# Spacing the score maxima of the early heads in an attention and feed-forward kernel on one core

## The chip, the cores and the metric

The kernel runs on one core of one Trainium2 chip. The metric is the device time of one execution in microseconds, from the runs' own clock; a profile of one more execution tells where the time lies.

## What is computed

Four batches of eight heads (768 positions, 64 values each) go through attention with a hashed mask: six sign bits of q and of k by a random projection give a bucket each, and a score counts only where the buckets agree. The heads' outputs, side by side, go through a feed-forward layer of 512 to 2048 to 512 with a piecewise quadratic activation.

```python
q_bits = (np.einsum('bhsd,dk->bhsk', q, proj) > 0)
mask = q_bucket[:, :, :, None] == k_bucket[:, :, None, :]
scores = np.where(mask, scale * np.matmul(q, k.transpose(0, 1, 3, 2)), -1000000000.0)
scores = scores - np.max(scores, axis=-1, keepdims=True)
attn = np.exp(scores)
attn = attn / (np.sum(attn, axis=-1, keepdims=True) + 1e-09)
x = np.matmul(attn, v)                       # 32 heads, then 3072 tokens x 512
h = x @ w_in
g = np.where(h >= 1, h, np.where(h <= -1, 0.0, (h + 1) ** 2 / 4))
out = g @ w_out
```

## The kernel before

All products are made from float32 values split into a high and a low part in TensorE's faster float32 format. Attention comes first, the feed-forward layer after it; the order of all work is written out by hand, so each engine and each DMA queue works through its instructions in the order of the program.

Attention runs over 384 units, twelve for each of 32 heads. A unit (number g) is one block of 128 keys against one half (384) of the queries of a head: unit g belongs to head g // 12, to half 0 in its first six units and half 1 in the others. In each pass of the main loop (from L609) TensorE makes the scores of unit g (`s_unit`, two matmuls, L371 and L372, into one of four score banks `ps_s`), ScalarE takes the exponential twice (L380, L385), VectorE or, for two of six blocks, GpSimd takes the difference of the two as the low part (`lo_unit`, for unit g - 1), and TensorE adds the product with the values of unit g - 4 (`pv_unit`, three matmuls, L404 to L406, into `obank[0]` or `obank[1]`). So a unit is five matmuls of 128x384. Two heads form a pair, whose operands `T1` and `T2` are in one of three sets. A row of `T2` holds the negative maximum of each query, and the bits of the hash, so that mask and maximum are part of the scores' second matmul, L372.

The maxima of a head are found before: six times, for 128 queries each, two matmuls (`max_mm`, L310) write a tile `smax` of two banks, of which there is one only, and VectorE reduces it (`max_red`, L314) in the next pass, behind `s_unit`. Where they stand is in the table `early` (L604 to L608) for heads 0 to 5, up to unit 47; from unit 48 on one is made in every even unit, for the head two further on, always at the end of the unit. When a head's six are there, they are clamped (`max_clamp`), transposed on TensorE into `obank[1]` (`max_tr`), copied by ScalarE and sent by DMA to their row of `T2` (`max_put`, L356) and, as flags, to DRAM (L357). For head 2 this is done in two halves (`half_clamp`, `half_put`, L337 and L338; put at units 19 and 25), whose first needs the first three maxima alone. Heads 0 and 1 get their rows in another way (`row_half`).

All large DMAs are issued by SyncE, in the order of the program. Around the change these are, for each pair: the load of the next pair's raw q and k (`load_raw`, L147), four moves between `T1` and `T2` (`move`, L163), the load of v (`load_v`, L286), four small DMAs of the bits (`bits_put`, L282), and the results of a head (L416, L417). For pair 2 the first two moves stand at unit 16, the third at 19, `load_raw` for pair 3 at 20, the fourth move and `load_v` at 24, `bits_put` at 25. For pair 3, made while heads 2 and 3 run, GpSimd splits the raw values at units 26 to 29 (`cast_h`, `low_h`), the moves are at 29 and 32, `load_raw` at 33. From pair 4 on (g0 the first unit of the pair two before it): split at g0 to g0 + 3, moves at g0 + 3 and + 6, `load_raw` at + 7, bits on TensorE (`bits_mm`, L210, eight matmuls) at + 7 and + 11, `bits_put` at + 18; there max_put stood at g0 + 5 for the odd head (as head 5 at unit 53) and at g0 + 17 for the even one (head 6 at 65). Conversions of the feed-forward weights are spread over the units too.

Of the kernel before, what the change touches and what calls it, by code (L numbers as in the profile page):

```python
# [110 lines left out]
NU = 2 * NJ  # L111


def attention(ctx, tc, wst, T1, T2, qk, v, pj, cv, x_d, s_d, e_d, tasks, shared):
# [148 lines left out]
    def row_half(hd, hf, bank=None):  # L263
        ps = ps_m.tile([P, 2, 512], F32, name="smax")[:, 0] if bank is None else obank[bank]
        row_mm(hd, hf, ps)
        nc.scalar.copy(out=T2[0][32:33, 0, hd, hf * HS:(hf + 1) * HS], in_=ps[32:33, 0:HS])
# [54 lines left out]
    def half_clamp(hd, hf):  # L321

        nm = nms[hd]
        x = nm[:, hf * HB:(hf + 1) * HB]
        nc.vector.tensor_scalar(out=nmh[:, hf, HB:2 * HB], in0=x, scalar1=CLAMP, scalar2=None, op0=ALU.is_gt)
        nc.vector.tensor_scalar(out=nmh[:, hf, 0:HB], in0=x, scalar1=CLAMP, scalar2=None, op0=ALU.min)

    def half_put(hd, hf, bank):
        pr, h = hd // 2, hd % 2
        if hf == 1:  # L330
            nms.pop(hd)
        ps = obank[bank]
        nc.tensor.transpose(out=ps[0:2 * HB, 0:P], in_=nmh[:, hf], identity=ident)
        te = small.tile([2 * NJ, P], F32R, name="te")[0:2 * HB]
        nc.scalar.copy(out=te, in_=ps[0:2 * HB, 0:P])
        sl = slice(hf * HS, (hf + 1) * HS)
        nc.sync.dma_start(out=T2[pr % NQK][7:8, 0, h, sl].bitcast(F32), in_=te[0:HB].bitcast(F32))  # L337
        nc.sync.dma_start(out=e_d[hd // H][hd % H:hd % H + 1, sl], in_=te[HB:2 * HB].bitcast(F32))  # L338
# [8 lines left out]
    def max_tr(hd, bank):  # L347
        ps = mx[hd] = obank[bank]
# [46 lines left out]
    def pv_unit(n):  # L395
# [8 lines left out]
        nc.tensor.matmul(out=o, lhsT=wa, rhs=ph, start=(jj == 0), stop=False)  # L404
        nc.tensor.matmul(out=o, lhsT=wb, rhs=ph, start=False, stop=False)  # L405
        nc.tensor.matmul(out=o, lhsT=wa, rhs=pl, start=False, stop=(jj == NJ - 1))  # L406
# [126 lines left out]
    at(9, ones_row, 1, nc.vector)  # L533
# [5 lines left out]
    at(7, row_clamp, 1, 0, NJ // 2)  # L539
# [3 lines left out]
    at(9, bits_cmp, 1, 0)  # L543
    at(9, row_half, 1, 0)
# [18 lines left out]
    at(18, half_clamp, 2, 0)  # L563
    at(19, half_put, 2, 0, 1)
    at(23, half_clamp, 2, 1)
    at(25, half_put, 2, 1, 0)
    at(2 * NU + 1, lambda: nc.gpsimd.memset(T2[0][32:33, 0].bitcast(F32), 0.0))
    for hd in range(NH):
        pr, h = hd // 2, hd % 2
        g = hd * NU  # L570
        if 0 < hd < NH - 2:
            gc, gt = ((g + NU + 6, g + NU + 7) if hd == 1 else (g + NU + 2, g + NU + 4) if hd == 2
                      else (g + NU, g + NU + 4))
            at(gc, max_clamp, hd + 2, nc.gpsimd if hd > 2 else nc.vector)
            at(gt, max_tr, hd + 2, 1)
            at(gt + (hd > 1), max_put, hd + 2)
# [27 lines left out]
    early = {}  # L604
    for hd, gs in ((0, (0, 2)), (1, (4, 5, 6, 8, 11, 12)), (2, (15, 16, 17, 19, 20, 22)),
                   (3, (21, 23, 24, 26, 27, 29)), (4, (30, 31, 33, 34, 35, 37)),
                   (5, (38, 39, 41, 42, 44, 46))):
        early.update({n: (hd, NJ - len(gs) + i) for i, n in enumerate(gs)})  # L608
    for g in range(NG + LAG + 1):  # L609
        if g < NG:  # L610
            s_unit(g)
        if red is not None:
            max_red(*red)
            red = None
        if 1 <= g <= NG:
            lo_unit(g - 1)
        if g < 4 * NU:
            due = g in early
            hd, i = early.get(g, (0, 0))
        else:  # L620
            hd, i = g // NU + 2, g % NU // 2
            due = hd < NH and g % 2 == 0
        if g >= LAG and g - LAG < NG:
            pv_unit(g - LAG)
        if due:
            max_mm(hd, 2 * i)
            max_mm(hd, 2 * i + 1)
            red = (hd, i)
        for fn, a in tasks.pop(g, ()):
            fn(*a)  # L630
    for g in sorted(tasks):
# [652 lines left out]
```

## Time and profile before

| | us |
|---|---|
| median of 3 runs | 981.41 |
| lowest and highest run | 980.84, 982.14 |
| profiled execution, from the first to the last instruction | 980.2 |
| TensorE busy in it | 966.7 (99%) |
| VectorE, ScalarE, GpSimd busy | 793.9, 679.6, 346.3 |

The profiled execution's span is 1.2 us under the median of the runs, which is what lies around it. Attention takes the first 460 us or so, the feed-forward layer the rest. In the profile PE is TensorE, PEld its loading of weights, DVE VectorE, ACT ScalarE, POOL GpSimd and SPq the queue of SyncE. A matmul's printed duration (0.34 us for 384 columns) overlaps the next one's: they follow each other at about half of it. The clock granted to TensorE is at its full level throughout.

### The profile page before, as it was taken

How to read it: one execution, taken by the hardware profiler on the slowest of the kernel's cores; microseconds unless marked ns; L12 is line 12 of the kernel's file. 1: busy time of each engine (PE TensorE's matmuls, PEld its weight loads, DVE VectorE, ACT ScalarE, POOL GpSimd, SP SyncE). 2: the span in 40 equal slices, each digit the busy share in tenths (PEclk: the TensorE clock that was granted, in tenths of full speed). 3: DMA queues.
4: the chain of work that ended last, by engine and by line, in shares of the span. 5: the costliest groups of instructions: out<-in, count | busy, mean ns of one | idle time of the engine just before them, and what ended most of it. 6: DMA issues, size and time to landing. Idle time of an engine off the chain costs nothing.

```text
span 980.2 us, 15590 instructions
## 1 busy us (share of the span) xinstructions
PE 966.7 (99%) x5050; PEld 889.7 (91%) x5050; DVE 793.9 (81%) x1359; ACT 679.6 (69%) x1481; POOL 346.3 (35%) x418
## 2 busy tenths in 40 slices
PE   8999999999999999999999999999999999999998
PEld 7889999999999999999999998888988889988886
DVE  8779999999999999887898887877866777655554
ACT  7878988898899898888655555455564545544444
POOL 8767777778887777666000000000000000000000
PEclk9999999999999999999999999999999999999999
DMA  6674667676666667644395478966458554454431
GB/s 164 178 189 108 165 175 184 192 180 192 168 159 162 177 174 187 161 119 126 126 319 185 129 237 287 314 223 205 116 157 240 149 183 119 143 159 119 117 88 65
DMA packets 95113, 167.56 MB, mean 171 GB/s; under 512 B 13956, under 2 KB 51960, under 8 KB 95032
## 3 DMA queue, kind: packets, MB, share of 16 engines
q1 hardware_dynamic: 94808, 166.56, 59.6%
q8 instruction: 40, 0.66, 0.3%
q14 instruction: 41, 0.34, 0.1%
q10 hardware_dynamic: 224, 0.00, 0.0%
HBM read 106.13 MB, written 33.87 MB: 143 GB/s over the span
## 4 chain that ended last, share of the span: by engine, by line
PE 87%; DVE 5%; ACT 3%; DMA 2%; issue 1%; POOL 1%; SPq 1%; DVEq 0%; ACTq 0%; POOLq 0%
PE y L822 27%; PE h L1054 18%; PE smax L310 7%; PE h L959 7%; PE o L406 5%; PE o L404 5%; PE o L405 5%; PE s L371 5%; PE s L372 5%; DVE nm L314 2%; PE o L210 2%; DVE pl L39 1%; DMA wraw<-in_w_in_dram 1%; ACT ph L380 1%; DMA sm<-sd 0%
## 5 line engine op out<-in xcount | busy, mean ns | idle before, releaser
L380 ACT ACTIVATE ph<-s 128x384 fp32r<-128x384 f32 x380 | 188.3, 496 | 41.1 <-PE s L372 35.1
L314 DVE TENSOR_REDUCE nm<-smax 128x1 f32<-128x768 f32 x189 | 179.0, 947 | 15.2 <-PE smax L310 13.6
L39 POOL TENSOR_TENSOR pl<-pf,ph 128x384 fp32r<-128x384 f32 x128 | 141.9, 1112 | 87.8 <-ACT pf L385 83.1
L787 DVE SCALAR_TENSOR_TENSOR t<-t 128x384 f32<-128x384 f32 x128 | 71.3, 557 | 101.6 <-ACT z L782 101.3
L39 DVE TENSOR_TENSOR pl<-s,ph 128x384 fp32r<-128x384 f32 x256 | 135.8, 544 | 10.8 <-ACT s L385 9.6
L371 PE MATMUL s<-t 128*128 128x384 f32 x384 | 132.2, 344 | 0.0
L404 PE MATMUL o<-ph,va 128*128 128x386 f32 x384 | 130.1, 339 | 1.1 <-DVE neg L221 1.1
L406 PE MATMUL o<-pl,va 128*128 128x386 f32 x384 | 130.1, 339 | 0.4 <-DVE pl L39 0.4
L405 PE MATMUL o<-ph,vb 128*128 128x386 f32 x384 | 130.1, 339 | 0.0
L372 PE MATMUL s<-t 128*128 128x384 f32 x384 | 129.3, 337 | 0.0
L385 ACT ACTIVATE s<-s 128x384 f32<-128x384 f32 x252 | 125.2, 497 | 0.0
L822 PE MATMUL y<-t,ghi 128*128 128x512 f32 x384 | 124.7, 395 | 0.0
L310 PE MATMUL smax<-t 128*128 128x384 f32 x378 | 103.1, 354 | 5.7 <-DVE nm L314 4.4
L781 ACT ACTIVATE t<-h,mh 128x384 f32<-128x384 f32 x56 | 32.6, 581 | 84.0 <-PE h L959 44.3
L310 PEld LDWEIGHTS smax<-t 128*128 128x128 f32 x378 | 64.4, 188 | 23.8 <-DVE nm L314 22.1
L792 ACT CAST ghi<-z 128x384 fp32r<-128x384 f32 x129 | 65.1, 505 | 30.1 <-DVE z L788 26.3
L782 ACT ACTIVATE z<-t,m 128x384 f32<-128x384 f32 x128 | 79.0, 617 | 4.2
L1054 PE MATMUL h<-wbig,t 128*128 128x384 f32 x399 | 81.4, 336 | 0.0
L822 PEld LDWEIGHTS y<-t,ghi 128*128 128x128 f32 x384 | 71.3, 188 | 11.1 <-ACT ghi L792 0.3
L1054 PEld LDWEIGHTS h<-wbig,t 128*128 128x128 f32 x399 | 71.6, 188 | 5.3
L781 ACT ACTIVATE t<-wsq,mh 128x384 f32<-128x384 f32 x48 | 29.6, 617 | 67.0 <-DVE wsq L1067 40.8
L822 PE MATMUL y<-t,glo 128*128 128x512 f32 x192 | 76.0, 396 | 0.0
(189 smaller groups left out, 2134.9 us busy)
## 6 DMA issues: line engine op xcount, KB each, us to landing
t<-wc SPq DMA_DIRECT2D x92, 256.0 KB
t<-t SPq DMA_DIRECT2D x60, 384.0 KB
wraw<-wc SPq DMA_DIRECT2D x76, 256.0 KB
raw<-in_qk_dram SPq DMA_DIRECT2D x14, 768.0 KB
wraw<-in_w_in_dram SPq DMA_DIRECT2D x16, 512.0 KB
wraw<-in_w_out_dram SPq DMA_DIRECT2D x16, 512.0 KB
t<-ed SPq DMA_DIRECT2D x36, 192.0 KB
xd<-xs SPq DMA_DIRECT2D x32, 192.5 KB
```

The lines of the kernel that those rows point to most:

```text
L39: eng.tensor_tensor(out=out, in0=a, in1=b, op=ALU.subtract)
L310: nc.tensor.matmul(out=smax[hd][:, hf, 0:HS], lhsT=t2[:, 0, h, i * P:(i + 1) * P], rhs=t2[:, 1, h, hf * HS:(hf + 1) * HS], start=True, sto ...
L314: nc.vector.tensor_reduce(out=nmp(hd)[:, i:i + 1], in_=smax[hd][:, :, 0:HS], axis=AX.XY, op=ALU.max, negate=True)
L371: nc.tensor.matmul(out=ps[:, 0:HS], lhsT=t1[:, 1, h, ks], rhs=t1[:, 0, h, sl], start=True, stop=False)
L372: nc.tensor.matmul(out=ps[:, 0:HS], lhsT=t2[:, 1, h, ks], rhs=t2[:, 0, h, sl], start=False, stop=True)
L380: nc.scalar.activation(out=ph[:, 0:HS], in_=ps[:, 0:HS], func=AF.Exp, scale=SCALE)
L385: nc.scalar.activation(out=pf, in_=ps[:, 0:HS], func=AF.Exp, scale=SCALE)
L404: nc.tensor.matmul(out=o, lhsT=wa, rhs=ph, start=(jj == 0), stop=False)
L405: nc.tensor.matmul(out=o, lhsT=wb, rhs=ph, start=False, stop=False)
L406: nc.tensor.matmul(out=o, lhsT=wa, rhs=pl, start=False, stop=(jj == NJ - 1))
L822: nc.tensor.matmul(out=ys[c][m], lhsT=g_[:, m * P:(m + 1) * P], rhs=w, start=(first and k == 0), stop=(last and k == 2))
L1054: nc.tensor.matmul(out=ps, lhsT=w[:, cs], rhs=x, start=(n == 0 and s not in (2, 3, 6)), stop=(n == 5), skip_group_check=True)
```

## The change

The maxima of heads 0 to 5 are placed by a count of matmuls, five for a unit, and no longer by units only: `between(k)` is called behind the scores and behind each of the three value matmuls, and makes a maximum where `early` names the place 5 g + k. Those of heads 2 to 5 begin at place 80 (unit 16) and stand 7.7 places apart, up to unit 51; those of later heads keep one in two units, four units later than before (`SHIFT`). A maximum inside a unit is reduced at once, one at its end behind the next `s_unit`, as before.

The rows of heads 2 to 4 are now made in halves (clamps at units 19, 24, 29, 34, 38, 43, puts at 21, 26, 31, 36, 40, 45), clamped by GpSimd and no longer by VectorE; those of later heads are transposed at g + 18 and put at g + 19, counted from the first unit g of the head two before, in place of g + 16 and g + 17. Transposes and the row of head 1's first half go to a tile of the score banks and no longer to `obank` or `smax`. `ones_row` comes behind the compare of the bits in unit 9, a clamp of head 1 one unit later.

```diff
+SHIFT = 4
     def row_half(hd, hf, bank=None):
-        ps = ps_m.tile([P, 2, 512], F32, name="smax")[:, 0] if bank is None else obank[bank]
+        ps = ps_s.tile([P, 512], F32, name="s") if bank is None else obank[bank]
...
-        nc.vector.tensor_scalar(out=nmh[:, hf, HB:2 * HB], in0=x, scalar1=CLAMP, scalar2=None, op0=ALU.is_gt)
-        nc.vector.tensor_scalar(out=nmh[:, hf, 0:HB], in0=x, scalar1=CLAMP, scalar2=None, op0=ALU.min)
+        nc.gpsimd.tensor_scalar(out=nmh[:, hf, HB:2 * HB], in0=x, scalar1=CLAMP, scalar2=None, op0=ALU.is_gt)
+        nc.gpsimd.tensor_scalar(out=nmh[:, hf, 0:HB], in0=x, scalar1=CLAMP, scalar2=None, op0=ALU.min)
-    def half_put(hd, hf, bank):
+    def half_put(hd, hf):
...
-        ps = obank[bank]
+        ps = ps_s.tile([P, 512], F32, name="s")
...
-    def max_tr(hd, bank):
-        ps = mx[hd] = obank[bank]
+    def max_tr(hd, bank=None):
+        ps = mx[hd] = ps_s.tile([P, 512], F32, name="s") if bank is None else obank[bank]
...
         nc.tensor.matmul(out=o, lhsT=wa, rhs=ph, start=(jj == 0), stop=False)
+        between(3)
         nc.tensor.matmul(out=o, lhsT=wb, rhs=ph, start=False, stop=False)
+        between(4)
         nc.tensor.matmul(out=o, lhsT=wa, rhs=pl, start=False, stop=(jj == NJ - 1))
...
-    at(9, ones_row, 1, nc.vector)
...
-    at(7, row_clamp, 1, 0, NJ // 2)
+    at(8, row_clamp, 1, 0, NJ // 2)
...
     at(9, bits_cmp, 1, 0)
+    at(9, ones_row, 1, nc.vector)
...
-    at(18, half_clamp, 2, 0)
-    at(19, half_put, 2, 0, 1)
-    at(23, half_clamp, 2, 1)
-    at(25, half_put, 2, 1, 0)
+    for hd, gs in ((2, (19, 21, 24, 26)), (3, (29, 31, 34, 36)), (4, (38, 40, 43, 45))):
+        for n, g in enumerate(gs):
+            at(g, half_put if n % 2 else half_clamp, hd, n // 2)
...
-        if 0 < hd < NH - 2:
-            gc, gt = ((g + NU + 6, g + NU + 7) if hd == 1 else (g + NU + 2, g + NU + 4) if hd == 2
-                      else (g + NU, g + NU + 4))
-            at(gc, max_clamp, hd + 2, nc.gpsimd if hd > 2 else nc.vector)
-            at(gt, max_tr, hd + 2, 1)
-            at(gt + (hd > 1), max_put, hd + 2)
+        if 2 < hd < NH - 2:
+            at(g + NU + SHIFT - 1, max_clamp, hd + 2, nc.gpsimd)
+            at(g + NU + SHIFT + 2, max_tr, hd + 2)
+            at(g + NU + SHIFT + 3, max_put, hd + 2)
...
-    early = {}
-    for hd, gs in ((0, (0, 2)), (1, (4, 5, 6, 8, 11, 12)), (2, (15, 16, 17, 19, 20, 22)),
-                   (3, (21, 23, 24, 26, 27, 29)), (4, (30, 31, 33, 34, 35, 37)),
-                   (5, (38, 39, 41, 42, 44, 46))):
-        early.update({n: (hd, NJ - len(gs) + i) for i, n in enumerate(gs)})
+    order = [(0, 4), (0, 5)] + [(hd, i) for hd in range(1, 6) for i in range(NJ)]
+    places = [5, 15] + [25, 33, 40, 48, 55, 62] + [80 + 77 * n // 10 for n in range(4 * NJ)]
+    early = {n + (n % 5 == 1): hi for n, hi in zip(places, order)}
+    for hd in range(6, NH):
+        early.update({5 * ((hd - 2) * NU + SHIFT + 2 * i + 1): (hd, i) for i in range(NJ)})
     for g in range(NG + LAG + 1):
+
+        def between(k):
+            if 5 * g + k in early:
+                hd, i = early.pop(5 * g + k)
+                max_mm(hd, 2 * i)
+                max_mm(hd, 2 * i + 1)
+                if k == 5:
+                    return hd, i
+                max_red(hd, i)
+
         if g < NG:
             s_unit(g)
         if red is not None:
             max_red(*red)
...
             lo_unit(g - 1)
+        between(2)
         if g >= LAG and g - LAG < NG:
-            pv_unit(g - LAG)
-        if due:
-            max_mm(hd, 2 * i)
-            max_mm(hd, 2 * i + 1)
-            red = (hd, i)
+            pv_unit(g - LAG, between)
+        red = between(5)
```

## Rows read from the trace of the kernel before

**Rows 1.** The page, busy time of TensorE: us, share of the span, instructions.
```profile
PE 966.7 (99%) x5050; PEld 889.7 (91%) x5050; DVE 793.9 (81%) x1359; ACT 679.6 (69%) x1481; POOL 346.3 (35%) x418
```
**Rows 2.** Busy time by stretch: units 12 to 23, 24 to 47, 48 to 71.
```profile
28.50:46.80 18.30, 17.28 (x94) 14.89 (x93) 14.54 (x25) 14.60 (x34) 12.80 (x16) 1.00 0.64 152
46.80:79.80 33.00, 30.49 (x165) 27.66 (x164) 26.65 (x40) 25.36 (x60) 18.20 (x20) 1.00 0.66 170
79.80:107.70 27.90, 27.81 (x156) 26.50 (x155) 26.71 (x39) 25.15 (x61) 21.07 (x24) 1.00 0.63 166
```
**Rows 3.** Waits of TensorE from 29 to 80 us: sum, times, longest, us.
```profile
PE smax L310 <- DVE nm L314: 3.5, 13, 1.1
```
**Rows 4.** Timeline of TensorE, units 29 to 30: start, duration, what, idle before.
```profile
54.98 0.34 PE L406 MATMUL o<-pl,va 128*128 128x386 f32 x1
55.49 0.61 PE L310 MATMUL smax<-t 128*128 128x384 f32 x2 [0.18 <-DVE nm L314]
55.94 0.34 PE L371 MATMUL s<-t 128*128 128x384 f32 x1
```
**Rows 5.** Timeline of VectorE, units 9 to 10 and 30 to 31.
```profile
24.61 0.70 DVE L191 MEMSET t<- 1x768 f32 x1 [0.19 <-PE smax L260]
25.34 0.55 DVE L221 TENSOR_TENSOR neg<-o,neg 32x384 f32<-32x384 f32 x1
...
55.82 0.87 DVE L342 TENSOR_SCALAR nm<-nm 128x6 f32<-128x6 f32 x1
...
57.05 0.95 DVE L314 TENSOR_REDUCE nm<-smax 128x1 f32<-128x768 f32 x1
```
**Rows 6.** Timeline of TensorE, unit 10 and the first unit of head 2 (24).
```profile
25.94 0.44 PE L404 MATMUL o<-ph,va 128*128 128x386 f32 x1 [1.05 <-DVE neg L221]
...
47.00 0.34 PE L372 MATMUL s<-t 128*128 128x384 f32 x1
```
**Rows 7.** Timeline of SyncE's queue, DMAs issued in units 15 to 22.
```profile
32.85 0.52 SPq L163 DMA_DIRECT2D t<-t  x1
...
36.56 0.52 SPq L163 DMA_DIRECT2D t<-t  x1
...
41.55 1.13 SPq L337 DMA_DIRECT2D t<-te  x1
...
44.02 0.59 SPq L147 DMA_DIRECT2D raw<-in_qk_dram  x1
```
**Rows 8.** DMA packets from 44.6 to 45.6 us, and from 49.1 to 49.5 us.
```profile
DMA packets 69, 0.22 MB, mean 221 GB/s; under 512 B 22, under 2 KB 34, under 8 KB 69
...
DMA packets 4, 0.02 MB, mean 46 GB/s; under 512 B 1, under 2 KB 1, under 8 KB 4
```
**Rows 9.** The page, DMA issues: what, times, size of one.
```profile
t<-t SPq DMA_DIRECT2D x60, 384.0 KB
...
raw<-in_qk_dram SPq DMA_DIRECT2D x14, 768.0 KB
```
**Rows 10.** Timeline of GpSimd, units 25 to 31.
```profile
49.56 1.38 POOL L567 MEMSET t<- 1x1536 f32 x1
...
56.60 0.51 POOL L152 CAST t<-raw 128x384 fp32r<-128x384 f32 x1
```
**Rows 11.** Timeline of SyncE's queue, units 55 to 70.
```profile
88.49 1.16 SPq L163 DMA_DIRECT2D t<-t  x2
...
92.63 0.50 SPq L163 DMA_DIRECT2D t<-t  x1
...
103.96 3.33 SPq L282 DMA_DIRECT2D t<-bits  x4
```
**Rows 12.** Timeline of TensorE, the first L372 of heads 5 and 6.
```profile
94.89 0.34 PE L372 MATMUL s<-t 128*128 128x384 f32 x1
...
107.91 0.33 PE L372 MATMUL s<-t 128*128 128x384 f32 x1
```
**Rows 13.** Timeline of TensorE near the end of attention, unit 376.
```profile
454.89 0.44 PE L406 MATMUL o<-pl,va 128*128 128x386 f32 x1 [0.36 <-DVE pl L39]
```

## What I expect the change to do to the time

> **What bounds the kernel now.** I began with the page: TensorE is busy for 966.7 of the 980.2 us, at a granted clock of 1.00 in every stretch that I read [rows 1, 2]. So only two things move the time: matmuls added or removed (none here) and time in which TensorE waits. I then read the stretches. From unit 48 on, 156 instructions take 27.90 us, one each 0.179 us. In units 24 to 47 there are 165 in 33.00 us (0.200), in units 12 to 23 there are 94 in 18.30 us (0.195). At 0.179 these would have taken 29.5 and 16.8 us: 3.5 and 1.5 us are lost, 5.0 in all [rows 2]. The list of waits names the loss: 13 times TensorE waited for the reduction of the maxima before [rows 3]. The timeline shows one such wait [rows 4]: L406 starts at 54.98, the next matmul at 55.49 and not at 55.16, and the pair after it takes 0.45 us and not 0.36. That is 0.42 us in all, though the printed idle time is 0.18, because a matmul's end overlaps the next one's start.
>
> This loss is what the spacing can win. A maximum needs two matmuls and 7.7 others, 9.7 x 0.179 = 1.74 us from one to the next; a cycle through the single two-bank tile takes 0.61 us for the pair [rows 4] and 0.95 us for its reduction [rows 5], 1.56 us. So it fits, with less than 0.2 us left for VectorE being late.
>
> **Part by part, up to unit 24.** The compare at 25.34 stands behind a memset of 0.70 us [rows 5]; `ones_row` now comes behind it, so that the wait of 1.05 us at unit 10 [rows 6] shrinks by about 0.9. Of the 1.5 us lost in units 12 to 23 I give back 1.2. Maxima up to unit 24 are 14 in place of 16, which moves 4 x 0.179 = 0.7 us to later. With 0.5 us for head 1's maxima (they too are spaced now), unit 24 could begin about 3.3 us earlier, its second matmul at 43.7 in place of 47.00 [rows 6].
>
> It can't, by the queue of SyncE. That second matmul (L372) reads the first half row of head 2, which a DMA brings. Before, the row (L337) is issued at 41.55, ahead of the pair's last move and of the 768 KB load of `raw` at 44.02 [rows 7, 9]. `half_put` moves from unit 19 to 21; the last move of the pair stays at 19 and `load_raw` at 20. So the row is now issued behind both. What that means is in the packets: 12 of 512 bytes (34 under 2 KB less 22 under 512 B; the row and the flags have 6, the flags of head 1 the other 6) run between 44.6 and 45.6, some three microseconds after issue, behind the moves that had been issued just before. Then the last move and the load follow, whose last large packets are still running between 49.1 and 49.5 [rows 8]. The queue's order is the order of arrival. The row would thus come behind those last packets; with about 0.5 us for completion, 50.0 at the old pace. What feeds this queue starts with the bits of pair 1, whose compare comes only a few tenths earlier, since a reduction now precedes it; I take 0.4 us off for this and 0.3 for the two small DMAs that are no longer ahead: 49.3 to 50.0, taken 49.7. TensorE then idles from 43.7 to 49.7, and stands 2.7 us later at this matmul than before. The ends: 0 (the row is there in time, first rival) and 50.5.
>
> [...]
>
> **Units 24 to 47.** Now 120 matmuls of units, 30 of 15 maxima, 8 of bits and 5 transposes: 163 x 0.179 = 29.2 us. To it I add 0.05 us for each of the 15 maxima (0.7), and a new wait at unit 31: head 3's clamp goes to GpSimd, behind three of the four casts of units 26 to 28. They begin after a memset at 49.56 that itself follows unit 24, and the fourth cast starts at 56.60, 9.6 us after unit 24's L372 [rows 6, 10]. The clamp takes its place there and ends 0.5 us later, so 59.8 in the new time; the transposition at the end of unit 31 would be due at about 58.8 (49 matmuls x 0.179 after 49.7, and a few short waits): 1.0 us. In sum 30.9 us in place of 33.0, so unit 48 starts 2.7 - 2.1 = 0.6 us later than before. By then 29 maxima are done in place of 32; three come later, 6 x 0.179 = 1.1 us. Taking `max_clamp` off VectorE (0.87 us of the slow row [rows 5]) is in these figures. The halves of heads 3 and 4 add two transpositions, two copies and four DMA issues; ScalarE and SyncE have room.
>
> **The steady part, 22 heads from 5 to 26.** Maxima stay at the same even units, so VectorE's load is as before. The row is now issued two units later. For an odd head this is behind the pair's third move, for an even one behind the four DMAs of the bits (unit 67 behind unit 66). The even head: the bits are issued from 103.96 to 107.29, 3.33 us for four with waits between them, and the row is needed at 107.91 [rows 11, 12]. Before, they stood behind the row, whose two issues cost some 1.2 us; without it the last of them is out at about 106. From issue to landing I take 1.9 us: a move of 384 KB issued at 32.85 lets the next be issued at 36.56, 3.7 us later [rows 7, 9], of which 1.8 are the transfer, at 0.22 MB in 1.0 us [rows 8]. That gives 107.9, just when it is needed. The odd head: three moves behind each other from 88.49, the third at 92.63 [rows 11]; with the clamp no longer ahead of the casts on GpSimd they start up to 1 us earlier. With 3.7 us for the first and 1.8 for each behind it the third ends at about 94.8; the row, behind it, is needed at 94.89 [rows 12]. Both lie within 0.3 us of zero. A wait can't be negative, so I take 0.1 each, 2.2 us; the ends are 0 and 0.5 each (11 us). The transposition in a score bank takes one of four banks for a unit: 0 to 0.1 us each; I take 0, and see nothing that it could win.
>
> **The end.** Three maxima less early are paid above; the last ones now fall in units 360 and 362, ahead of a stretch in which TensorE already waits for VectorE (at 454.89) [rows 13]. Two reductions are 1.9 us of VectorE against 0.7 us more of TensorE; 0.7 us of waiting is my middle (0 to 1.2).
>
> **The sum.** 980.2 + 0.6 + 1.1 + 2.2 + 0.7 = 984.8 us of span; the median of the runs lies 1.2 us over the profiled span, so 986.0 us.
>
> **The rivals.** First, the faster end: the row of head 2 is in time, because the load of `raw` does not hold it up. Then unit 24 starts the 3.3 us earlier, units 24 to 47 take 29.9 us in place of 33.0 without the wait on GpSimd, and 1.1 and 0.7 come back later: 980.2 - 3.3 - 3.1 + 1.1 + 0.7 = 975.6 of span, with the 2.2 of the later rows 977.8, so 976.8 to 979.0. For it: before, the row was in time with two moves ahead of it; against it: the packets come in order, and the load's last ones run beyond 49. It decides if the row's packets are through by 43.7.
>
> [...]
>
> Third, beyond the forecast: every row of heads 5 to 26 is late by 0.5 us, 8.8 us more: 994.8. Its place is the first L372 of each head, its price what the row's landing lies past 94.89 and 107.91 in the pair shown [rows 12]; it decides once the third move ends 0.4 us later than I worked out. That the change does not do what it says, spacing without shorter waits since VectorE is late, gives up the 2.1 us of units 24 to 47: 988, inside the forecast's range.
>
> **How the numbers follow.** Forecast 0.53, first rival 0.17, second 0.22, third 0.08. Range: from 977.5 (over half of the first rival) to 992.0 (part of the third), which leaves out 0.14; the forecast's own is 983.5 to 990, by a wait at unit 24 up to 0.8 longer or 1.5 shorter and the later rows at 0 to 0.25 each. Faster 0.17, same 0.23, slower 0.60.
>
> **What would show it.** Right: an idle time of 4 to 6 us ahead of the first L372 of head 2, ended by a DMA; the load of `raw` ahead of the row in SyncE's timeline; an idle time ahead of head 3's first transposition, ended by GpSimd; few waits for the reductions in units 12 to 51; idle times of some tenths ahead of the first L372 of later heads. Wrong: no wait at unit 24, or waits for the reductions as before.

## The result, and the profile after

The changed kernel takes 986.26 us (median; runs from 985.59 to 987.82) against 981.77 us for the kernel before beside it: 1.0044 times the time, 95% interval 1.0029 to 1.0058. It is slower, by what the forecast said (986.0). The profiled execution took 985.59 us, the quickest of them, and its span is 983.8 us.

From here on L372 and L373 are the two scores matmuls of a unit (one line further than before), L311 those of a maximum, L338 the issue of a half row, L405, L407 and L409 the products with the values. In the runs made from the kernel before (e5, e6, e14) the lines are those of the kernel before.

First the page: the busy time of the engines, and the costliest groups, with the idle time ahead of them and what ended it.

```profile
PE 963.2 (98%) x5052; PEld 891.6 (91%) x5052; DVE 779.2 (79%) x1351; ACT 679.3 (69%) x1483; POOL 354.8 (36%) x430
...
L373 PE MATMUL s<-t 128*128 128x384 f32 x384 | 131.2, 342 | 8.3 <-DMA t<-te 8.2
```

Then TensorE's list of waits over the whole span (us in total, times, longest):

```profile
PE s L373 <- DMA t<-te: 8.2, 13, 4.0
...
PE o L211 <- ACT xs L415: 1.3, 1, 1.3
PE smax L311 <- DVE nm L315: 1.2, 3, 0.6
PE o L409 <- DVE pl L39: 0.8, 3, 0.4
```

The spacing did what it says: where TensorE waited 13 times for the reduction of the maxima in units 12 to 47 [rows 3], it now does so 3 times in the whole span, and in none of these units. A wait that was not in this list before has taken its place, for the DMA of the rows, 13 times. The list over 80 to 410 us, heads 5 and on, holds 12 of them:

```profile
PE s L373 <- DMA t<-te: 4.2, 12, 0.9
PE smax L311 <- DVE nm L315: 0.6, 1, 0.6
```

so the other 4.0 us are one wait. It stands in TensorE's timeline at unit 24, the first of head 2 (start, duration, what; in brackets the idle time before it and what ended it):

```profile
44.38 0.96 PE L211 MATMUL o<-t,pw 128*128 128x384 f32 x4 [1.26 <-ACT xs L415]
45.18 0.33 PE L372 MATMUL s<-t 128*128 128x384 f32 x1
49.53 0.69 PE L373 MATMUL s<-t 128*128 128x384 f32 x1 [4.01 <-DMA t<-te]
50.01 0.52 PE L405 MATMUL o<-ph,va 128*128 128x386 f32 x1
50.33 0.53 PE L407 MATMUL o<-ph,vb 128*128 128x386 f32 x1
...
53.24 0.34 PE L373 MATMUL s<-t 128*128 128x384 f32 x1
53.42 0.34 PE L405 MATMUL o<-ph,va 128*128 128x386 f32 x1
```

The reader sees three things: a smaller wait of 1.26 us just before (for a copy of ScalarE), the wait for the row, and matmuls that follow each other at 0.32 us instead of 0.175 until about 53. The stretches answer to [rows 2] (us, then busy time of PE, PEld, DVE, ACT, POOL with their instructions; the granted clock; the DMA engines' share; GB/s):

```profile
45.20:49.50 4.30, 0.32 (x2) 0.00 (x0) 2.34 (x4) 1.27 (x4) 1.30 (x3) 0.60 0.85 242
49.50:53.20 3.70, 3.67 (x12) 3.68 (x13) 0.70 (x1) 2.51 (x5) 1.88 (x2) 0.54 0.82 194
53.20:79.60 26.40, 26.40 (x153) 25.35 (x152) 22.14 (x33) 22.33 (x56) 18.99 (x29) 1.00 0.56 148
```

The granted clock, 1.00 in the stretches of before, is 0.60 while TensorE waits and 0.54 in the 3.7 us behind. After that, up to unit 48, it is 1.00 again and TensorE is never idle.

Where the time went is best read from the start of each unit (its L372) in the two traces. The table holds, for this kernel and for all that follow, by how much each stretch of units is longer than in the kernel before, from one profiled execution each. Five of these kernels (the changed one, e1, e3, e10 and e12) have the same code from unit 48 to 348 and read 1.8 to 3.0 there, so that two single readings of this column that differ by less than a microsecond tell nothing; the five with the rows a unit earlier read 0.8 to 1.0.

| units | 12-24 | 24-25 | 25-48 | 48-348 | 360-372 |
|---|---|---|---|---|---|
| changed kernel | -0.92 | +4.57 | -3.18 | +2.22 | +1.64 |
| e1, load behind the row | -0.66 | +1.33 | +2.60 | +1.83 | +1.64 |
| e2, later rows a unit earlier | -1.02 | +4.80 | -2.65 | +0.91 | +0.60 |
| e4, both | -0.62 | +0.69 | +2.78 | +0.81 | +0.60 |
| e3, long fill | +4.27 | -0.34 | -2.82 | +3.01 | +1.63 |
| e10, short fill | +4.37 | -0.26 | -2.86 | +1.77 | +1.64 |
| e7, other early order | -2.45 | +2.34 | +0.19 | +0.80 | +1.67 |
| e12, own queue | -0.72 | +4.42 | -2.32 | +2.33 | +1.63 |
| e13, own queue and e2 | -0.94 | +4.68 | -1.63 | +0.99 | +0.59 |
| e15, e13 and memset earlier | -1.07 | +5.22 | -1.35 | +1.03 | +1.67 |
| e5, before with the late half row | +2.32 | +0.75 | -0.07 | -0.12 | 0.00 |
| e6, before with late rows | -0.04 | 0.00 | 0.00 | +17.00 | +0.92 |
| e14, the same, score bank | -0.01 | 0.00 | 0.00 | +4.67 | +1.25 |

In the changed kernel unit 48 starts 0.25 us earlier than before: the wait at unit 24 eats nearly all that the spacing wins. The loss is made behind unit 48: 2.2 us up to unit 348, most of it by the later rows, and 1.6 at the end.

### The profile page after: what moved, and what is told of

It reads as the page before. It is cut to its first block, busy times and chain, and to the rows that moved or that the text cites. A ratio compares the mean times of both kernels' runs of the same rounds, so it can differ in the third digit from the quotient of the medians.

```text
span 983.8 us, 15542 instructions
## 1 busy us (share of the span) xinstructions
PE 963.2 (98%) x5052; PEld 891.6 (91%) x5052; DVE 779.2 (79%) x1351; ACT 679.3 (69%) x1483; POOL 354.8 (36%) x430
## 4 chain that ended last, share of the span: by engine, by line
PE 80%; DMA 8%; ACT 7%; DVE 3%; issue 2%; POOL 0%; SPq 0%; ACTq 0%; DVEq 0%; POOLq 0%
PE y L824 27%; PE h L1056 18%; PE h L961 7%; DMA t<-te 6%; PE smax L311 5%; PE s L373 5%; PE o L405 4%; PE o L409 4%; PE o L407 4%; PE s L372 4%; ACT ph L381 2%; DMA vraw<-in_v_dram 1%; ACT s L386 1%; ACT pf L386 1%; DVE pl L39 1%
## 5 line engine op out<-in xcount | busy, mean ns | idle before, releaser
L39 POOL TENSOR_TENSOR pl<-pf,ph 128x384 fp32r<-128x384 f32 x128 | 138.9, 1089 | 82.3 <-ACT pf L386 82.2
L373 PE MATMUL s<-t 128*128 128x384 f32 x384 | 131.2, 342 | 8.3 <-DMA t<-te 8.2
L372 PE MATMUL s<-t 128*128 128x384 f32 x384 | 132.5, 345 | 0.0
L409 PE MATMUL o<-pl,va 128*128 128x386 f32 x384 | 130.5, 340 | 0.8 <-DVE pl L39 0.8
L405 PE MATMUL o<-ph,va 128*128 128x386 f32 x384 | 130.4, 340 | 0.6 <-DVE neg L222 0.6
L407 PE MATMUL o<-ph,vb 128*128 128x386 f32 x384 | 130.4, 339 | 0.0
L311 PE MATMUL smax<-t 128*128 128x384 f32 x378 | 99.5, 344 | 2.6 <-DVE nm L315 1.2
L794 ACT CAST ghi<-z 128x384 fp32r<-128x384 f32 x129 | 65.1, 505 | 30.1 <-DVE z L790 26.3
L373 PEld LDWEIGHTS s<-t 128*128 128x128 f32 x384 | 72.6, 189 | 12.9 <-DMA t<-te 12.7
L311 PEld LDWEIGHTS smax<-t 128*128 128x128 f32 x378 | 67.2, 189 | 10.1 <-DVE nm L315 7.4
```

The source lines that it names most:

```text
L39: eng.tensor_tensor(out=out, in0=a, in1=b, op=ALU.subtract)
L311: nc.tensor.matmul(out=smax[hd][:, hf, 0:HS], lhsT=t2[:, 0, h, i * P:(i + 1) * P], rhs=t2[:, 1, h, hf * HS:(hf + 1) * HS], start=True, sto ...
L372: nc.tensor.matmul(out=ps[:, 0:HS], lhsT=t1[:, 1, h, ks], rhs=t1[:, 0, h, sl], start=True, stop=False)
L373: nc.tensor.matmul(out=ps[:, 0:HS], lhsT=t2[:, 1, h, ks], rhs=t2[:, 0, h, sl], start=False, stop=True)
```

## The experiments

### Where the wait at unit 24 comes from: e1, e5, e12

**e1** takes the bulk out of the row's way: the pair's third move and the load of raw stand behind the first half row.

```diff
-            at(g0 + 6, move, pr + 2, 2)
+            at(g0 + (6 if pr else 9), move, pr + 2, 2)
-                at(g0 + 7, load_raw, pr + 3)
+                at(g0 + (7 if pr else 9), load_raw, pr + 3)
```

> The changed kernel with one thing more: pair 2's third move and the load of raw for pair 3 are put at unit 22, behind the first half row of head 2 (unit 21), and no longer at 19 and 20. If the wait of 4.0 us at head 2's first L372 comes from the order of the DMAs, the row now lands behind two moves only, at about 46.4 us: a wait of about 1 us is left, no low clock follows, unit 48 starts some 3 to 4 us earlier than in the changed kernel, and the time is 981.5 to 983.5 us. Rival: the row is late because it is made late (clamp on GpSimd, transposition in a score bank, copy behind ScalarE's wait for v): the wait stays at 3 us or more and the time at 985.5 to 986.5.

Measured: 987.54 us, ratio 1.0053 (1.0035 to 1.0071). The row now has the DMA engines nearly to itself (their busy share is 0.01 from 45.2 to 46.8), and the wait at unit 24 is down from 4.0 to 0.8 us. The clock fell all the same, against the expectation: it is 0.50 from 46.8 to 48.7, behind this wait and one of 1.5 us just before (for ScalarE's copy). But the load is only pushed on to the second half row, which unit 30 needs:

```profile
59.34 0.44 PE L373 MATMUL s<-t 128*128 128x384 f32 x1 [3.97 <-DMA t<-te]
```

So the bulk is the cause of the wait, the rival (a row made late) alone is not, and the expected gain went into the next row. Units 24 to 48 together are 3.9 us longer than before; in the changed kernel 1.4.

**e5** is the kernel before, with the first half row put out at unit 21 and no other edit.

```diff
-    at(19, half_put, 2, 0, 1)
+    at(21, half_put, 2, 0, 1)
```

> The kernel before, with the first half row of head 2 put out at unit 21 instead of 19, and nothing else: on SyncE it now stands behind the pair's last move and the load of raw, as in the changed kernel. If the order on SyncE alone makes the wait at unit 24, the row lands at 49.5 to 50.3, TensorE waits 2.5 to 3.5 us ahead of the second matmul of unit 24 (which was at 47.00), matmuls right behind it run at a granted clock under 0.8 for some 3 us, and the time is 2.5 to 4.5 us over the kernel before: 984.5 to 986.5. If the wait comes from the other parts of the change (the spacing, the clamp on GpSimd), the row is there by 47.0 and the time stays within 0.5 us of before.

Measured: 985.24 us, ratio 1.0031 (1.0020 to 1.0042), so the time is as expected, but the wait is not the one expected. TensorE's timeline, and below it VectorE's:

```profile
45.55 0.44 PE L404 MATMUL o<-ph,va 128*128 128x386 f32 x1 [2.14 <-DVE neg L221]
...
50.05 0.45 PE L372 MATMUL s<-t 128*128 128x384 f32 x1 [0.47 <-DMA t<-te]
```

```profile
44.95 0.55 DVE L221 TENSOR_TENSOR neg<-o,neg 32x384 f32<-32x384 f32 x1 [2.48 <-ACT te L335]
```

The row lands at 50.0, as worked out, and TensorE stands 3 us late at this matmul. But it lost 2.1 of them earlier: in the kernel before the transposition uses an `obank`, ScalarE empties it late, the compare of the bits waits for that and the next value matmul for the compare. The bank is the one in which the bits stand: two units later the transposition comes between their matmuls and their compare and writes over a corner of them, so this run tells of times only, and is no kernel to use. The transposition in a score bank, which the change brings along, avoids both.

**e12** sends the half rows from ScalarE, on a queue that carries nothing else from unit 0 on.

```diff
     def half_put(hd, hf):
-        nc.sync.dma_start(out=T2[pr % NQK][7:8, 0, h, sl].bitcast(F32), in_=te[0:HB].bitcast(F32))
+        nc.scalar.dma_start(out=T2[pr % NQK][7:8, 0, h, sl].bitcast(F32), in_=te[0:HB].bitcast(F32))
```

> The changed kernel, with the DMA of the half rows of heads 2 to 4 issued by ScalarE, behind its copy of the row, and so on a queue of its own; the bulk stays where it is on SyncE. If the row of head 2 is late because of its place behind the load of raw in SyncE's queue, it lands some 2 us after its issue, the waits ahead of units 24 and 30 are under 1 us each (4.0 us at unit 24 in the changed kernel), no low clock follows, unit 48 starts 1.5 to 2.5 us before that of the kernel before, and since the later rows (1.7 us) and the end (1.6 us) stay as in the changed kernel, the time is 982.5 to 984. If the sixteen DMA engines themselves are the limit, whatever the queue, the row still lands near 49.5, the wait stays 3 us or more, and the time 985.5 to 986.5.

Measured: 986.61 us, ratio 1.0064 (1.0048 to 1.0081): no gain, if anything a loss (0.9 us of it in units 25 to 48, and 1.0 in e13 against e2). The wait is still there, 3.85 us (in this profiled execution, as in those of e7 and e10, all from unit 10 on stands 3 us later, for a reason told in the last section):

```profile
53.15 0.69 PE L373 MATMUL s<-t 128*128 128x384 f32 x1 [3.85 <-DMA t<-te]
```

ScalarE's timeline gives the issue:

```profile
46.01 0.83 ACT L290 CAST va<-vraw 128x768 fp32r<-128x768 f32 x1 [2.22 <-DMA vraw<-in_v_dram]
...
47.98 0.25 ACT L336 CAST te<-s 6x128 fp32r<-6x128 f32 x1
48.26 0.79 ACTq L338 DMA_DIRECT2D t<-te  x1
```

From issue to the matmul that was waiting it is 4.9 us (48.26 to 53.15), in the changed kernel on SyncE's queue 5.05 (44.48 to 49.53), in e1, with no bulk just ahead of it, 1.8 (44.91 to 46.72). So neither the place in SyncE's queue nor the queue at all makes the 5 us; the large transfers issued shortly before do, through whichever queue. The packets show it: from the row's issue to its first packet SyncE's queue (q1) moves 0.95 MB, and the six packets of the row on ScalarE's queue run from 51.84 to 52.48, 3.6 to 4.2 us after issue. The second half row of this run, issued at 58.88 with no move or load under way, has all six between 60.15 and 60.30, 1.3 us after issue, so ScalarE's queue is not slow in itself. Packets by queue, from 48.26 to 51.84 and from 60.15 to 60.30:

```profile
q1 hardware_dynamic: 186, 0.95, 95.6%
...
q10 hardware_dynamic: 6, 0.00, 4.5%
```

Of the two expectations that of a limit which both queues share holds. Whether it is the DMA engines themselves or something ahead of them is not shown.

The second thing is why the issue is late. TensorE's timeline in the changed kernel (the transposition of the row), then ScalarE's and SyncE's:

```profile
40.75 0.27 PE L334 MATMUL s<-ident,nmh 128*6 128x128 f32 x1
```

```profile
42.23 0.83 ACT L290 CAST va<-vraw 128x768 fp32r<-128x768 f32 x1 [2.04 <-DMA vraw<-in_v_dram]
...
43.84 0.48 ACT L415 COPY xs<-o 128x384 f32<-128x384 f32 x1
44.20 0.25 ACT L336 CAST te<-s 6x128 fp32r<-6x128 f32 x1
```

```profile
41.85 0.87 SPq L164 DMA_DIRECT2D t<-t  x1
42.76 0.64 SPq L148 DMA_DIRECT2D raw<-in_qk_dram  x1
44.48 0.77 SPq L338 DMA_DIRECT2D t<-te  x1
```

The row is transposed by 41.0, but copied only at 44.20; SyncE is done with the load at 43.4 and then waits for the copy. That copy stood ahead of the cast of v before; moved two units, it stands behind it, and the cast waits 2.04 us for the DMA of v. The copy of a finished half head (L415) stands there too, and TensorE's wait of 1.26 us at 44.38 is for it. So the row's issue moved by 2.9 us (from 41.55 [rows 7] to 44.48) through two queues, ScalarE's and SyncE's.

### What the low clock costs: e3 and e10

Both add matmuls of 256 columns, whose results nobody uses, at the end of unit 23, so that TensorE is not idle while the row is on its way: 30 in e3, 16 in e10.

```diff
+    def fill():
+        ps = ps_m.tile([P, 2, 512], F32, name="smax")[:, 0]
+        for _ in range(30):
+            keep_busy(ps)
+
+    at(23, fill)
```

> The changed kernel with 30 more matmuls of 256 columns on zeros at the end of unit 23, which only keep TensorE at work while the first half row of head 2 is under way. The row lands when it did (about 49.5), since TensorE does not decide that. If the ten matmuls after the wait, 0.32 us apart in place of 0.175, are slow because of the clock granted after an idle stretch (0.54 in the rows from 49.5 to 53.2 us), they are at full pace now, and the time falls by 1 to 1.6 us to 984.7 to 985.3. Rival: their pace is set by something else that waits with the row: it stays, and so does the time, 986.3.

> The changed kernel, with 16 extra matmuls of 256 columns (2 us of TensorE, results unused) at the end of unit 23, so that TensorE is busy in most of the time in which it waits for the half row, and done before the row lands at 49.5. If the slow matmuls behind the wait come from the clock, the matmuls from 50 to 53 us follow each other at 0.17 to 0.18 us and not 0.32, units 25 to 30 are 1.0 to 1.6 us shorter than in the changed kernel, and the time is 984.6 to 985.5. If the time is unchanged although the pace is restored (986.0 to 986.5), later waits take it up.

Measured: e3 988.66 us, ratio 1.0068 (1.0046 to 1.0089); e10 986.36 us, 1.0041 (1.0026 to 1.0056). The fill of e3, and then that of e10, in the timeline and with its stretch:

```profile
47.04 3.85 PE L426 MATMUL smax<-idle 128*128 128x256 f32 x30 [1.45 <-DVE nm L315]
50.74 0.33 PE L372 MATMUL s<-t 128*128 128x384 f32 x1
50.91 0.34 PE L373 MATMUL s<-t 128*128 128x384 f32 x1
```

```profile
48.46 0.96 PE L211 MATMUL o<-t,pw 128*128 128x384 f32 x4 [1.50 <-ACT xs L415]
50.86 3.64 PE L426 MATMUL smax<-idle 128*128 128x256 f32 x16 [1.44 <-DVE nm L315]
54.30 0.42 PE L372 MATMUL s<-t 128*128 128x384 f32 x1
54.56 0.34 PE L373 MATMUL s<-t 128*128 128x384 f32 x1
```

```profile
50.80:54.30 3.50, 3.44 (x16) 3.44 (x17) 0.92 (x3) 0.00 (x0) 0.44 (x2) 0.54 0.80 229
```

The fill of e3 was too long: it runs past the landing, and there is no wait left at L373. Its matmuls are 0.128 us apart and those behind it 0.17, at a granted clock of 1.00 from 47.0 to 56.0. In e10 the fill itself ran at the low clock, 0.54 in its stretch, 0.228 us each (3.64 / 16), after two waits of 1.5 us in 4 us; what came behind it ran at 0.99 (54.3 to 60.0). So the slow matmuls are the clock and nothing in their operands. The price: in the changed kernel units 24 to 30 are 5.2 us longer than before, 1.0 more than the wait (4.17, from L372 to L373 less the usual step); in e3, with no wait, 0.3 shorter. That makes 1.4 us. Yet units 30 to 48 give back 3.8 us in the changed kernel and 2.8 in both filled ones, which show the wait that the forecast had at unit 31 ("PE s L334 <- POOL nmh L327", 0.8 us each). In the changed kernel this wait is not there. So it seems that the low clock gave GpSimd the time to be ready, and that net it cost some 0.4 us; e10 came out at the second of its two expectations, no gain. e3's expectation of the time is missed by the length of its fill for 1.0 us (unit 48 starts 0.74 later than before, in the changed kernel 0.25 earlier); 0.8 more lie in units 48 to 348, within what that column scatters.

### The rows of heads 5 and on: e2, e6, e14

**e2** puts these rows one unit earlier, ahead of the third move and of the bits.

```diff
-            at(g + NU + SHIFT + 2, max_tr, hd + 2)
-            at(g + NU + SHIFT + 3, max_put, hd + 2)
+            at(g + NU + SHIFT + 1, max_tr, hd + 2)
+            at(g + NU + SHIFT + 2, max_put, hd + 2)
```

> The changed kernel, with the transposition and the DMA of the rows of heads 5 to 31 one unit earlier each, which puts the row ahead of the pair's third move (odd heads) and ahead of the bits (even heads) again; the maxima stay where the change put them. If the later heads' waits for their rows come from that order, the 12 waits at a later head's first L372 (4.2 us by the list of waits, about 6 us from start to start) are gone, and the stretch from unit 52 to 348 is 1.5 to 2 us shorter, as much as it grew: 984.3 to 985.0 us. Rival one: the rows are late because the maxima are; then the waits stay and the time is 986.3. Rival two: the waits only take the place of waits for reductions, which come back: 985.5 to 986.3 with the waits gone.

Measured: 984.15 us, ratio 1.0022 (1.0009 to 1.0035), at the lower end of what was expected. Its list of waits over 80 to 410 us:

```profile
PE s L350 <- POOL nm L345: 1.9, 8, 0.3
PE smax L311 <- DVE nm L315: 1.9, 4, 0.6
```

The 12 waits for the DMA are gone. New ones stand for them: the transposition now waits for GpSimd's clamp, eight times, and the waits for reductions come back. Units 48 to 348 lose 0.9 us instead of 2.2. So the gross waits (4.2 us) were never the net price: where TensorE does not stand for a row, it stands for VectorE or GpSimd instead.

**e6** and **e14** are the kernel before with these rows two units later; in e14 the transposition also goes to a score bank.

```diff
-            at(gt, max_tr, hd + 2, 1)
-            at(gt + (hd > 1), max_put, hd + 2)
+            late = 2 if hd > 2 else 0
+            at(gt + late, max_tr, hd + 2, 1)
+            at(gt + late + (hd > 1), max_put, hd + 2)
 # e14 only
-        ps = mx[hd] = obank[bank]
+        ps = mx[hd] = ps_s.tile([P, 512], F32, name="s") if hd > 4 else obank[bank]
```

> The kernel before, with the transposition and the row of heads 5 to 31 two units later, so that on SyncE the row stands behind the third move (odd heads) or the bits (even heads), as in the changed kernel; the maxima stay where they were. If this order is what the later rows cost, the first matmul of some 10 to 20 of these heads that reads the row waits 0.3 to 1.2 us, 4 to 10 us together; VectorE catches up in these waits, so that the time rises by less, 1.5 to 4 us: 983.5 to 986. If the later rows cost nothing by themselves, there are no such waits and the time is 981.5 to 982.5.

> The kernel before, with the rows of heads 5 to 31 two units later, as in an earlier run, but their transposition in a score bank and no longer in the bank that the bits' matmuls of those units use. If the 17 us of that run came from the bank (bits matmuls waiting for ScalarE's copy of the transposed maxima), they are gone; what is left is the place of the row behind the third move or the bits on SyncE: waits of 0.3 to 1.2 us ahead of 10 to 20 heads and 983 to 985.5. If the 17 us come from the later rows themselves, the time stays above 990.

Measured: e6 999.42 us, ratio 1.0176 (1.0161 to 1.0192); e14 987.46 us, 1.0068 (1.0054 to 1.0081). The lists over 80 to 410 us, e6 and then e14:

```profile
PE o L210 <- ACT te L354: 18.6, 11, 1.7
```

```profile
PE s L372 <- DMA t<-te: 8.6, 12, 0.9
```

Both expectations missed upwards, and e6 in kind: its 17 us are waits of the bits' matmuls for the bank in which the transposed maxima still stand. In a score bank they are gone, and what is left are the waits for the rows, 12 as in the changed kernel, but twice as long (8.6 us against 4.2) and 4.7 us net. One difference shows in the pair at 117 us: in e14, as in the kernel before, the clamp on GpSimd stands ahead of the pair's casts, and the third move is out 5.2 us before the head's first unit (117.72 to 122.92), in the changed kernel 5.5 (117.02 to 122.56). That it is the whole of the difference is not shown.

### Whether the parts add: e4, e7, e13, e15

**e4** is e1 and e2 in one. **e7** is e2 with the early bulk moved around the half rows:

```diff
-            at(g0 + 3, move, pr + 2, 0)
-            at(g0 + 3, move, pr + 2, 1)
-            at(g0 + 6, move, pr + 2, 2)
+            at(g0 + (3 if pr else 9), move, pr + 2, 0)
+            at(g0 + (3 if pr else 9), move, pr + 2, 1)
+            at(g0 + (6 if pr else 14), move, pr + 2, 2)
-                at(g0 + 7, load_raw, pr + 3)
+                at(g0 + (7 if pr else 6), load_raw, pr + 3)
-            at(g + n + 1, move, pr + 2, 3)
+            at(g + n + (1 if pr else 10), move, pr + 2, 3)
-            at(g + (18 if pr else 25), bits_put, pr + 2)
+            at(g + (18 if pr else 27), bits_put, pr + 2)
-            gv = g + LAG + (2 if pr else 16)
+            gv = g + LAG + {0: 19, 1: 5}.get(pr, 2)
```

> Both: pair 2's third move and the load of raw behind head 2's first half row, and the rows of heads 5 to 31 one unit earlier. If both causes are as said and add up: 979.5 to 981.5 us, at or under the kernel before (981.8), so that the spacing's own gain becomes visible. If the spacing itself wins nothing because VectorE is at its limit anyway: not under 982.5.

> The changed kernel, with the rows of heads 5 to 31 one unit earlier, and with the bulk of pair 2 moved around the half rows: the load of raw for pair 3 two units earlier (unit 19), moves 0 to 2 of pair 2 behind the first half row (units 22 and 27), bits and the fourth move behind the second half row (units 27 and 33), the loads and casts of v moved likewise. If what the change lost is the half rows of head 2 waiting in the queue of SyncE, the waits ahead of units 24 and 30 go below 1 us both, unit 48 starts 1.5 to 2.5 us before that of the kernel before, and the time is 979.5 to 981.5. If the transfers only shift their delay to yet another place (the moves needed for head 4 at unit 48, v at unit 24), a wait of 1 us or more appears there and the time is 983 or more.

Measured: e4 985.18 us, ratio 1.0031 (1.0019 to 1.0044); e7 983.83 us, 1.0021 (1.0006 to 1.0037), with runs from 980.86 to 987.47. The gains hoped for are missed in both, and the times lie where the second case of each expectation puts them (not under 982.5; 983 or more). In e4 the wait goes to unit 30, as in e1. In e7 two waits are left, the first at unit 24 again, since the load issued at 43.75 was still under way when the row was issued at 45.41; the second, of the half row of head 3, at unit 36:

```profile
50.21 0.44 PE L373 MATMUL s<-t 128*128 128x384 f32 x1 [2.40 <-DMA t<-te]
```

In all the orders tried here some half row stood behind bulk.

**e13** is e12 and e2 in one; **e15** is e13 with a memset of GpSimd (1.37 us) moved from unit 6 to the start, for the reason told in the last section.

```diff
+    nc.gpsimd.memset(T2[1][0:64, 0].bitcast(F32), 0.0)
     cast_v(0, nc.gpsimd)
-    at(6, lambda: nc.gpsimd.memset(T2[1][0:64, 0].bitcast(F32), 0.0))
```

> As the kernel with the half rows on ScalarE's queue, and the rows of heads 5 to 31 one unit earlier on SyncE. If the two costs of the change that were found so far (the queue at unit 24, the later rows) are separate, their gains add: 980.5 to 982.5, with what is left the 1.6 us at the end. If taking one away only brings up the next (waits for GpSimd's clamp, reductions), it is 983 or more.

> As the kernel with the half rows on ScalarE's queue and the later rows one unit earlier, and GpSimd's memset for pair 1 (1.37 us) taken from unit 6 to the start, where GpSimd waits 1.07 us for v. In two profiled executions VectorE's clamp at unit 9 took 4.12 us, up to the end of a GpSimd instruction, while GpSimd ran one instruction behind the other from 20.4 to 28 us. If GpSimd's run without a gap is what holds VectorE, the runs no longer spread over some 4 to 6 us, the clamp takes 0.3 to 1 us in each profile, and the median is 0.3 to 1.5 us under the kernel without this edit. If it is not, spread and median are the same within 0.5 us.

Measured: e13 985.14 us, ratio 1.0042 (1.0030 to 1.0055); e15 986.65 us, 1.0050 (1.0037 to 1.0064), runs from 984.79 to 988.04. The gains hoped for are missed again. e13, with 983 or more as in its second case, has e2's gain in the later rows and none at unit 24. In e15 the clamp at unit 9 takes 0.67 us, as hoped, but the hold-up has moved with the memset: VectorE's clamp ahead of unit 0, 0.17 us in e13, takes 0.93, up to the memset's end at 12.20. VectorE's timeline, then GpSimd's:

```profile
11.30 0.93 DVE L252 TENSOR_SCALAR nrow<-nm 128x3 fp32r<-128x3 f32 x1
```

```profile
10.82 1.38 POOL L518 MEMSET t<- 64x1536 f32 x1
```

Unit 0 begins 1.1 us later than in e13 and unit 12 still 1.0, and the spread is no smaller. None of these kernels is quicker than the kernel before.

## Why the prediction was right

**The loss that the spacing wins** was read rightly: the reductions' waits are gone, and units 12 to 48, 0.5 us longer than before with the wait of 4.2 us for the row, would be 3.7 shorter without it. Of these 1.1 are the three maxima that are made later and no gain. The prediction had 5.0 for this stretch; the difference is about the wait of 1.26 us, which it did not have. **The start of unit 24** was the first miss. It was put 3.3 us earlier and is 1.6 (12 to 24 won 0.9 of 1.9, and 0.7 of 1.4 came ahead of that; the wait at unit 10 shrank from 1.05 [rows 6] to 0.57 and not by 0.9). The step that failed is one that was left out: up to unit 24 the prediction followed SyncE's order only, and of ScalarE it says, for the halves of heads 3 and 4, that it has room. A moved step brings its place in ScalarE's order with it, and there the row's copy and L415 now stand behind a cast that waits for a DMA. The wait of 1.26 us at 44.38 is the result.

**The row's landing** was put at 49.7 and lies at 49.5, the wait (from L372 to L373) at 6.0 against 4.2, for the reason just told. The number was right and its reason half right. "The queue's order is the order of arrival" was the step; e1 shows that the bulk ahead of the row is the cause, but e12 shows that the order on SyncE's queue is not needed for it. Also most of the 5 us were there before the change: the row issued at 41.55 stood behind two moves then, and its packets were through by 45.6 [rows 7, 8], 4 us after issue. What the change moved was the issue, by 2.9 us, and the landing with it. No run shows the 0.5 us for completion that is in this sum; in e12 and e13 it is 0.7 from the row's last packet to the matmul that waited. The second rival, a row that lands a microsecond earlier, fell: the matmul that waited for it starts at 49.53.

**Units 24 to 48** were given 30.9 us from the row's landing; from L373 at 49.53 to unit 48 at 79.59 it is 30.1. A wait of 1.0 us for GpSimd at unit 31 was in the sum and a low clock was not. In the changed kernel, e3 and e10 they exclude each other: with the low clock there is no wait for GpSimd, and where the clock is kept behind unit 24 it comes, 0.8 us (in e7, with a wait of 2.4 us and a clock of 0.53 from 50.8 to 54.3, 0.45 of it is left). Two terms, one missing and one too many, cancelled, which is luck.

**Unit 48** was put 0.6 us later and is 0.25 earlier. **The later rows** were 0.1 us each, 2.2 in all: units 48 to 348 are 2.2 us longer, of which a third of a microsecond is the one maximum more that falls there, so that 1.9 are the rows'. The size is right, the shape is not: 12 waits of up to 0.9 us, nearly all ahead of odd heads, whose row stands behind the third move, and not 22 of 0.1. The third rival, 0.5 us at each of 22, is not reached even in e14, with 8.6 us gross and 4.7 net.

**The end**: 0.7 for two more maxima and 0.7 of waiting were in the sum, 1.4; measured 1.64. But e2, e4 and e13, the same there, have 0.60, and e14, with its maxima where they were, 1.25. So the two maxima cost 0.6, no more than their matmuls, and the waiting of 0.7 that was laid to their reductions comes from something else, 1.0 us in the changed kernel; the last section has it.

**"The transposition in a score bank ... see nothing that it could win"** was wrong: without it the late rows cost 17 us in e6 in place of 4.7 in e14, and 2.1 us in unit 22 in e5, where the bits are written over besides. The change needs it.

In sum the span came out at 983.8 instead of 984.8. The profiled execution was the quickest; the median of the runs lies 2.5 us above its span and not 1.2, so the median agrees to 0.3 us, closer than the steps do: the way of the loss was right, the last few tenths are luck.

## What to carry to other kernels

A small transfer that someone waits for should be costed by what bulk was issued in the few microseconds before it, on any queue: here 5 us from issue to use behind moves and loads, 1.8 with none just ahead; and taking the bulk away from one such row hands it to the next (in e1, 3.97 us at unit 30), so all of them are to be looked at together. When a step is moved, list its place in every engine's order, also in those that have room: here one cast on ScalarE, which waited 2.04 us for a DMA, held up the copy of the row behind it. Spacing that frees an engine pays only up to the next thing that has a fixed time, and one wait of 4 us in place of 13 of a few tenths is no gain, and here the clock fell to 0.50 in it besides.

## What was not expected of the hardware

**The granted clock** fell in the changed kernel in one wait of 4.0 us (0.70 from 45.2 to 47.3, 0.50 from 47.3 to 49.5), and stayed at 0.50 for the 3 us behind it, with matmuls at 0.32 us instead of 0.175. In e10 it was 0.54 (50.8 to 54.3) behind two waits of 1.50 and 1.44 us, with 0.96 us of matmuls between them; in e3, with waits of 1.15 and 1.45 us, it was 1.00 throughout (43.0 to 56.0). In e1 it was 0.50 (46.8 to 48.7) behind waits of 1.51 and 0.77 us, and in e4, with 1.56 and 0.76, 1.00 (45.2 to 53.2): the waits alone do not tell which it will be.

**VectorE and GpSimd seem to hold each other up.** VectorE's clamp at unit 9 takes 0.26 us in the changed kernel's profile. In the profiled executions of e7, e10 and e12 it took 4.1; e7's, VectorE's timeline and then GpSimd's:

```profile
22.75 4.12 DVE L252 TENSOR_SCALAR nrow<-nm 128x3 fp32r<-128x3 f32 x1
```

```profile
21.42 1.97 POOL L39 TENSOR_TENSOR t<-raw,t 128x384 fp32r<-128x384 f32 x2
23.34 1.37 POOL L540 MEMSET t<- 64x1536 f32 x1
24.68 0.98 POOL L39 TENSOR_TENSOR pl<-pf,ph 128x384 fp32r<-128x384 f32 x1
25.64 0.24 POOL L256 TENSOR_SCALAR nm<-nm 128x6 f32<-128x6 f32 x1
25.86 0.98 POOL L39 TENSOR_TENSOR pl<-pf,ph 128x384 fp32r<-128x384 f32 x1
```

It ends at 26.87, when GpSimd's instruction from 25.86 does, the fifth in a row without a gap since the clamp began. In e10 and e12 it ends with the same instruction. All behind it is 3 us later, and this is why the table above starts at unit 12. It is likely what spreads the runs of these kernels too: the three profiled executions with it are each the slowest run of their kernel. At the end of attention it seems that hundredths decide which of the two engines is the slow one. In the changed kernel GpSimd's difference started first, at 448.59, and VectorE's took 1.38 us:

```profile
448.67 1.38 DVE L704 TENSOR_TENSOR raw<-raw,t 128x384 f32<-128x384 f32 x1
```

In e13 the same instruction took 0.56 us, and GpSimd's, which began with it at 449.34, took 1.44 in place of 1.05:

```profile
449.35 0.56 DVE L704 TENSOR_TENSOR raw<-raw,t 128x384 f32<-128x384 f32 x1
```

The stretch from unit 360 to 372 is 1.0 us longer in the first case, with three waits for VectorE's low part in the whole span and not one. All seven kernels with 1.6 to 1.7 in that column have 1.37 to 1.41 us for this instruction, all three with 0.6 have 0.55 or 0.56. In e14 it is 0.54 beside 1.25, so that something else adds there, which is not explained. What makes one of the two engines stand is not shown. A run of GpSimd without a gap does not do it alone: in the changed kernel it had one instruction behind the other from 20.43 to 26.89 too, and VectorE's clamp at 22.18 took its 0.26 us.
